# The second step of a double visit moved one visit on, in an attention and SwiGLU kernel on one core

## The chip, the core and the metric

The kernel runs on one core of a Trainium2 chip. The metric is the time of one execution on the device in microseconds, as the median of several runs. The core's engines are named as in the profile: PE is TensorE (matrix products), ACT is ScalarE (activations), DVE is VectorE (elementwise), POOL is GpSimd, and SP is SyncE, which here issues DMAs. Matrix products go to PSUM, the accumulation memory, from which ACT and DVE take them to SBUF.

## The reference

Attention over 8 batches and 12 heads with 448 positions and head size 64, and then a gated feed-forward layer over the 3584 tokens, with width 768 and inner width 1536:

```python
def _attn_ref(q, k, v):
    scores = (1.0 / np.sqrt(q.shape[-1])) * np.matmul(q, k.transpose(0, 1, 3, 2))
    scores = scores - np.max(scores, axis=-1, keepdims=True)
    attn = np.exp(scores)
    attn = attn / (np.sum(attn, axis=-1, keepdims=True) + 1e-09)
    return np.matmul(attn, v)

def _moe_ref(x, w_gate, w_val, w_out):
    g = x @ w_gate
    silu = g * (1.0 / (1.0 + np.exp(-g)))
    val = x @ w_val
    return silu * val @ w_out
```

The input of the feed-forward layer is the attention's output, with the heads side by side.

## The kernel before, in words

The attention is worked off by pairs of heads, 48 of them (six to a batch). The order of the instructions on each engine is written out by hand: every engine takes them in the order in which the program issues them, and semaphores make an engine wait where a tile isn't ready or isn't free. From pair 6 on, the program is a list of *visits* (`plan`, loop over `x`). A visit issues

- the scores of three chunks of keys (`qk`, L356 and L368) into three tiles of the PSUM pool `ps_s`, and for each an exponential on ACT (L378),
- the products with the values for one earlier pair, `todo` (L462), into two tiles of the pool `ps_f`, with the division by the row sums on DVE (`pv_close`, L504 and L505), which writes the pair's slot of a ring of six tiles `xt`,
- the DMA transpose of that pair's result into `X`, the input of the feed-forward layer (`turn_x`, L550, and L556 for the remainder of two pairs),
- the preparation of a later pair's queries and keys (copies on POOL, L240, and a DMA transpose on SP, L244),
- and a share of the feed-forward work of earlier batches.

One visit in seven is *bare*: no pair is due and there are no products with values. The pool `ps_s` has three tiles, each of two banks, and `ps_f` has two of one bank each; a new tile takes the place of the oldest one and waits for its readers.

For the last 33 visits the feed-forward share comes from the table `VISITS`. Its columns are: a block of output work to begin, the number of steps, the number of pairs of output tiles (`run_group`), the number of plain outputs (`run_o`), and the number of sums on DVE (`add_sum`). Rows are numbered here from 0, and "visit 24" means row 24; rows 3, 10, 17, 24 and 31 are bare. A *step* works out 128 columns of the inner layer for one block of tokens, 512 in this part: six matmuls for the gate and six for the value (L610), tanh on ACT, and two multiplications on DVE, of which the last (L696) writes `hts`. A step can be issued in these ways:

- `run_fv`: whole, 512 columns at a time.
- `run_pair`: two steps woven into each other. In a bare visit the first gate goes to a tile of `ps_f` (`gate_small`) and the second to `ps_s`; the second step's value comes in two halves of 256.
- `halves`: gate and value in halves of 256 tokens. The two gate halves take the two banks of one `ps_s` tile, each half has its own tanh (L670) and its own multiplication (L675), and the two value halves take both `ps_f` tiles, each closed by its own L696.

In the loop over the visits, `lone` picks `halves`:

```python
lone = nf == 1 and bool(todo)
...
if lone:
    fvq.pop(0).halves()
    add_sum()
elif bare_next(x):
    for _ in range(nf):
        run_fv()
else:
    run_steps(nf)
```

A *quarter output* is one plain output tile of 128 tokens by 192 columns (`plain_out`, twelve matmuls, L732). It is moved out of PSUM by DVE (L740), or by ACT (L742) in visit 26 (`by_vector`); the last of the four stores the 768 columns. A group in visits 28 and 31 makes two output tiles of 128 tokens out of seven products (L759), after four sums on DVE for each (L593 to L596).

While steps of an old block are left, the transposes of pairs that belong to the next but one block are kept back (`held`), since they overwrite the `X` that those steps read. They are issued at the end of the visit in which the last step was issued. After the last visit, the feed-forward layer of the last four batches follows in units (L929), for which POOL forms sums of weights (L892 to L895) as soon as the attention's buffers come free.

Of the kernel before, what the change touches and what calls it, by code (L numbers as in the profile page):

```python
# [65 lines left out]
def kernel(  # L66
# [959 lines left out]
    with tc.manual_schedule():  # L1026
# [52 lines left out]
        def add_block(i, visits):  # L1079
            if i < B - 2 * NB:  # L1080
                f1, own, n = block(i)
                fvq.extend(f1)
                kk, c0, hts = own
            else:
                own = None
            t_out = NFB * OH / 2400.0
            if i == 0:
                oq.extend([(ffn2_steps(*own, by_half(range(n // 128), OH)), t_out)] * (2 * (n // 128)))
            if i < 2:
                if i:  # L1090
                    ffn2_wait.append(own)
                    sums.extend(wsums)
                    wsums.clear()
                return
            kk, c0, hts = ffn2_wait.pop()
            ffn2_wait.append(own)
            odd = i % 2 == 0
            new = [OutPair(kk, c0, hts, t, 1 - t if i == B - 2 * NB else t) for t in range(1 + odd)]
            groups.extend(new)
            if not odd:  # L1100
                w = QW
                oq.extend([(ffn2_steps(kk, c0, hts, by_half([2], w)), t_out)] * (DM // w))
            for pair in new:
                pair.todo = pair.sums()
                sums.extend(pair.todo)
# [10 lines left out]
        ]  # L1116

        def token_sums(x, w, t, eng=nc.vector):
# [128 lines left out]
        while g < last or queue:  # L1247
            n = 2 if g < WIDE * NC else 3
            todo = []
# [34 lines left out]
        for x, (chunks, todo) in enumerate(plan):  # L1284
# [9 lines left out]
            begins, nf, ng = VISITS[x - base][:3] if x >= base else (0, 0, 0)  # L1294
            if begins > 2:
                add_block(begins, 0)
            lone = nf == 1 and bool(todo)
            behind = []
            for n, (pr, c) in enumerate(ordered if x else []):
                if ng and not todo:  # L1300
# [76 lines left out]
            else:  # L1377
                begins, nf, ng, no, ns = VISITS[x - base]
# [178 lines left out]
```

## Time and profile before

| | us |
|---|---|
| median of 3 runs | 419.69 (419.47 to 420.2) |
| the profiled execution, by the clock of the runs | 420.08 |
| its span, first to last instruction | 418.3 |
| PE busy in the span | 412.2 (99%) |
| DVE, ACT, POOL busy | 273.7, 248.9, 225.4 |
| granted TensorE clock | 1.0 |

The page of the profile gives busy times of each engine and the chain of work that ended last. The timeline gives instructions in order of time, merged where they follow each other on one line of the program: start in microseconds from the start of the span, length, engine, line, operation, the tiles that it writes and reads, and in brackets the idle time before it and what ended that. PE's matmuls overlap, and their ends are modelled, so the distance between starts is the better measure. Visit 24 begins at 232.96 us, visit 31 at 260.17 us.

### The profile page before, as it was taken

How to read it: one execution, taken by the hardware profiler on the slowest of the kernel's cores; microseconds unless marked ns; L12 is line 12 of the kernel's file. 1: busy time of each engine (PE TensorE's matmuls, PEld its weight loads, DVE VectorE, ACT ScalarE, POOL GpSimd, SP SyncE). 2: the span in 40 equal slices, each digit the busy share in tenths (PEclk: the TensorE clock that was granted, in tenths of full speed). 3: DMA queues.
4: the chain of work that ended last, by engine and by line, in shares of the span. 5: the costliest groups of instructions: out<-in, count | busy, mean ns of one | idle time of the engine just before them, and what ended most of it. 6: DMA issues, size and time to landing. Idle time of an engine off the chain costs nothing.

```text
span 418.3 us, 10870 instructions
## 1 busy us (share of the span) xinstructions
PE 412.2 (99%) x4346; PEld 260.4 (62%) x4346; DVE 273.7 (65%) x630; ACT 248.9 (59%) x387; POOL 225.4 (54%) x346
## 2 busy tenths in 40 slices
PE   8999999999999999999999999999999999999996
PEld 3666666655587786786767676555555655555664
DVE  4767562567786674579646578766757665757763
ACT  6975677656677675787656695655453345454121
POOL 8856534998898986398976814599800000000000
PEclk9999999999999999999999999999999999999999
DMA  9999999999999999999999935600000430000225
GB/s 135 192 200 200 200 177 195 129 166 205 196 142 179 153 194 172 154 158 151 167 159 171 102 62 106 186 18 0 2 0 2 121 107 0 2 0 0 76 79 150
DMA packets 108195, 50.29 MB, mean 120 GB/s; under 512 B 60400, under 2 KB 104816, under 8 KB 108144
## 3 DMA queue, kind: packets, MB, share of 16 engines
q0 software_dynamic: 46848, 24.56, 48.3%
q1 hardware_dynamic: 61024, 24.79, 34.7%
q8 instruction: 34, 0.56, 0.6%
q10 hardware_dynamic: 272, 0.25, 0.2%
q14 instruction: 17, 0.14, 0.1%
HBM read 49.55 MB, written 11.01 MB: 145 GB/s over the span
## 4 chain that ended last, share of the span: by engine, by line
PE 94%; DVE 2%; ACT 2%; issue 1%; ACTq 0%; DVEq 0%
PE gp L610 14%; PE un L929 12%; PE vp L610 12%; PE og L759 11%; PE ub L929 10%; PE ob L759 8%; PE acc L462 8%; PE s L356 5%; PE op L732 4%; PE s L393 2%; PE acc L426 2%; PE s L368 1%; PE tp L324 1%; PE wp L166 1%; ACT E L403 1%
## 5 line engine op out<-in xcount | busy, mean ns | idle before, releaser
L378 ACT ACTIVATE E<-s 128x896 f16<-128x896 f32 x126 | 107.4, 916 | 38.2 <-PE s L356 28.0
L610 PE MATMUL gp<-X,wg 128*128 128x256 f16 (+3 forms) x402 | 61.7, 300 | 0.0
L610 PE MATMUL vp<-X,wv 128*128 128x256 f16 (+3 forms) x402 | 58.6, 289 | 0.4 <-DVE xt L505 0.4
L240 POOL COPY qk<-qkraw 128x512 f16<-128x512 f16 x70 | 43.5, 668 | 22.8 <-DMA qkT<-qk 21.7
L180 POOL DMA_DIRECT2D vraw<-in_v_dram x72 | 44.1, 637 | 14.8 <-DMA wo<-in_moe_w_out_dram 8.0
L610 PEld LDWEIGHTS <-wv 128*128 128x128 f16 x444 | 41.6, 98 | 15.3 <-DVE xt L505 0.9
L610 PEld LDWEIGHTS <-wg 128*128 128x128 f16 x402 | 35.5, 98 | 15.8 <-issue 2.2
L180 POOL DMA_DIRECT2D qkraw<-in_k_dram x70 | 42.7, 630 | 4.9 <-DMA wo<-in_moe_w_out_dram 3.5
L403 ACT ACTIVATE E<-s 112x896 f16<-112x896 f32 x48 | 40.7, 918 | 7.5 <-PE s L393 7.5
L462 PEld LDWEIGHTS <-E 128*128 128x128 f16 (+2 forms) x1224 | 38.2, 98 | 8.5 <-issue 3.1
L462 PE MATMUL acc<-vo,E 128*128 128x65 f16 (+2 forms) x1224 | 42.1, 193 | 0.1
L759 PEld LDWEIGHTS <-hts 128*128 128x128 f16 x282 | 27.1, 98 | 17.0
L690 DVE SCALAR_TENSOR_TENSOR t<-sg,gp 128x384 f32<-128x384 f32 (+1 forms) x29 | 17.4, 614 | 24.3 <-ACT sg L637 24.3
L696 DVE SCALAR_TENSOR_TENSOR hts<-t,vp 128x256 f16<-128x256 f32 (+3 forms) x67 | 30.9, 461 | 3.5 <-PE vp L610 1.2
L505 DVE TENSOR_TENSOR xt<-acc,R 128x256 f16<-128x256 f32 x72 | 30.6, 425 | 2.5
L203 POOL DMA_DIRECT2D qkraw<-in_q_dram x44 | 30.2, 685 | 3.0 <-PE s L393 1.0
L356 PE MATMUL s<-qkT 64*64 64x448 f16 (+1 forms) x288 | 28.5, 352 | 0.0
L1002 ACT ACTIVATE silu<-un 128x448 f32<-128x448 f32 x24 | 13.1, 544 | 21.7 <-PE un L929 20.0
L759 PE MATMUL og<-wo,hts 128*128 128x384 f16 x132 | 25.4, 326 | 0.0
L986 DVE TENSOR_TENSOR un<-ub,kept 128x448 f32<-128x448 f32 x24 | 15.1, 631 | 15.6 <-ACT kept L983 10.2
L990 DVE TENSOR_TENSOR kept<-ub,kept 128x448 f32<-128x448 f32 x24 | 15.0, 625 | 13.2 <-PE ub L929 13.2
L979 ACT ACTIVATE ub<-un 128x448 f32<-128x448 f32 x24 | 12.7, 529 | 15.4 <-PE un L929 13.9
(213 smaller groups left out, 748.2 us busy)
## 6 DMA issues: line engine op xcount, KB each, us to landing
vraw<-in_v_dram POOLq DMA_DIRECT2D x72, 64.0 KB, 5.1
qkraw<-in_q_dram POOLq DMA_DIRECT2D x41, 112.0 KB, 4.7
qkraw<-in_k_dram POOLq DMA_DIRECT2D x68, 64.0 KB, 5.0
out_dram<-osb SPq DMA_DIRECT2D x7, 336.0 KB, 3.3
wg<-in_moe_w_gate_dram POOLq DMA_DIRECT2D x8, 288.0 KB, 9.5
wv<-in_moe_w_val_dram POOLq DMA_DIRECT2D x8, 288.0 KB, 10.0
wo<-in_moe_w_out_dram POOLq DMA_DIRECT2D x2, 1152.0 KB, 18.0
out_dram<-osb SPq DMA_DIRECT2D x7, 288.0 KB, 4.9
```

The lines of the kernel that those rows point to most:

```text
L180: eng.dma_start(dst[ts(s, 64)], rows)
L203: nc.gpsimd.dma_start(dst, flat.rearrange("h (p c) d -> p h (c d)", c=NC))
L240: nc.gpsimd.tensor_copy(dst.rearrange("p c h d -> p h c d"), src)
L356: nc.tensor.matmul(s[ts(half, m), hx, 0:S].rearrange("p (c q) -> p c q", q=P), lhsT=t[ts(hx, 64), ds((c + low(pr, hx)) * 128 + half * m, m ...
L378: nc.scalar.activation(e, s[:, :, 0:S], AF.Exp, scale=sm_scale)
L403: nc.scalar.activation(e[:, :, 0:S], s[0:P, :, 0:S], AF.Exp, scale=sm_scale)
L462: nc.tensor.matmul(acc[ds(lo, m), ts((j + pr % 2) % (KR + 1), D + 1)], lhsT=e[rows, ds(hx * S + j * 128 + lo, m)], rhs=Vts[pr % NV][rows, ...
L505: nc.vector.tensor_tensor(xt[:, :, hx], a4[:, :, 0:D], r[:].unsqueeze(2).to_broadcast([128, KR + 1, D]), ALU.mult,)
L610: nc.tensor.matmul(dst[:, 0:w], lhsT=wslice(kind, self.fb, cb), rhs=X[kk][:, cb, ds(c0 + lo, w)], start=(cb == 0), stop=(cb == NCB - 1),)
L696: nc.vector.scalar_tensor_tensor(self.hts[:, self.fb, ds(lo, w)], self.t1[:, ds(lo, w)], 0.5 * HS, vp[:, 0:w], ALU.mult, ALU.mult)
L759: nc.tensor.matmul(dst, lhsT=lhs(n), rhs=rhs(n), start=first and n == 0, stop=n == NH - 1, skip_group_check=True)
L929: mm = nc.tensor.matmul(dst, lhsT=lhs[:, n], rhs=rhs[:, n], start=first and n == 0, stop=n == NK - 1, skip_group_check=True,)
```

## The change

In the table, visit 24 gets one step in place of two, and visit 25 gets the other. The block whose output pairs are used in visits 28 and 31 begins in visit 26 in place of 25, and the four quarter outputs, which were in visits 25, 26, 27 and 29, are now in 26, 27, 29 and 30. The four sums ahead of visit 28 are two in visit 26 and two in visit 27 (before: one, one and two). `lone` no longer asks for a pair that is due, so the single step of the bare visit 24 is issued by `halves` like that of visit 25. No other bare visit has a single step.

```diff
@@ VISITS, rows 20 to 32
             (0, 0, 1, 0, 0), (0, 1, 0, 0, 0), (0, 1, 0, 0, 0), (0, 1, 0, 0, 0),
-            (0, 2, 0, 0, 0),
-            (4, 0, 0, 1, 1), (0, 0, 0, 1, 1), (0, 0, 0, 1, 2), (0, 0, 1, 0, 0), (0, 0, 0, 1, 2),
-            (0, 0, 0, 0, 0), (0, 0, 1, 0, 0), (0, 0, 0, 0, 0),
+            (0, 1, 0, 0, 0),
+            (0, 1, 0, 0, 0), (4, 0, 0, 1, 2), (0, 0, 0, 1, 2), (0, 0, 1, 0, 0), (0, 0, 0, 1, 2),
+            (0, 0, 0, 1, 0), (0, 0, 1, 0, 0), (0, 0, 0, 0, 0),
         ]
@@ loop over the visits
             begins, nf, ng = VISITS[x - base][:3] if x >= base else (0, 0, 0)
             if begins > 2:
                 add_block(begins, 0)
-            lone = nf == 1 and bool(todo)
+            lone = nf == 1
             behind = []
```

2 rows, old and new, of the table VISITS are left out of this document.

## The prediction

> **What bounds the kernel now.** I read the head of the page first, then the timeline of TensorE over the visits that the change touches, then that of ScalarE, VectorE and SyncE beside it.
>
> ```profile
> span 418.3 us, 10870 instructions
> PE 412.2 (99%) x4346; PEld 260.4 (62%) x4346; DVE 273.7 (65%) x630; ACT 248.9 (59%) x387; POOL 225.4 (54%) x346
> PE 94%; DVE 2%; ACT 2%; issue 1%; ACTq 0%; DVEq 0%
> L378 ACT ACTIVATE E<-s 128x896 f16<-128x896 f32 x126 | 107.4, 916 | 38.2 <-PE s L356 28.0
> ```
>
> TensorE is busy for 99% of the span and is 94% of the chain that ended last. So whatever lengthens the stream of matmuls, or stops it, is paid in full; the other engines matter only where TensorE waits for them. An exponential (L378) takes 916 ns. The profiled execution took 420.08 us by the clock of the runs, 1.78 us outside its span of 418.3, and lies 0.39 us over the median of 419.69; I work out a difference from its rows and add it to the median.
>
> Now TensorE. Columns: start, length, engine, line and operation. The ends of matmuls are modelled, so I use distances between starts only.
>
> ```profile
> 228.71 0.74 PE L356 MATMUL s<-qkT 64*128 64x448 f16 x6
> 229.29 1.12 PE L462 MATMUL acc<-vo,E 64*128 64x65 f16 x32
> 230.24 1.47 PE L610 MATMUL gp<-X,wg 128*128 128x256 f16 x12
> 231.55 1.47 PE L610 MATMUL vp<-X,wv 128*128 128x256 f16 x12
> 232.96 0.38 PE L368 MATMUL s<-qkT 64*64 64x448 f16 x4
> 233.65 2.76 PE L610 MATMUL gp<-X,wg 128*128 128x512 f16 x12
> 236.25 1.46 PE L610 MATMUL vp<-X,wv 128*128 128x512 f16 x6
> 238.95 0.74 PE L356 MATMUL s<-qkT 64*128 64x448 f16 x6
> 239.53 1.12 PE L462 MATMUL acc<-vo,E 64*128 64x65 f16 x32
> 240.49 1.15 PE L732 MATMUL op<-wo,hts 128*128 128x192 f16 x12
> 241.57 0.38 PE L368 MATMUL s<-qkT 64*64 64x448 f16 x4
> 241.94 0.57 PE L356 MATMUL s<-qkT 64*64 64x448 f16 x8
> 242.32 1.16 PE L462 MATMUL acc<-vo,E 64*64 64x65 f16 x40
> 243.31 1.15 PE L732 MATMUL op<-wo,hts 128*128 128x192 f16 x12
> 244.40 0.85 PE L356 MATMUL s<-qkT 64*128 64x448 f16 x6
> 247.13 0.38 PE L368 MATMUL s<-qkT 64*64 64x448 f16 x4
> 258.50 0.88 PE L356 MATMUL s<-qkT 64*128 64x448 f16 x6
> 259.20 1.13 PE L462 MATMUL acc<-vo,E 64*128 64x65 f16 x32
> 260.17 1.14 PE L759 MATMUL og<-wo,hts 128*128 128x384 f16 x6
> ```
>
> The reader sees one visit after another, each beginning with scores (L356 or L368). Visit 23 begins at 228.71: scores 0.58, products of a pair 0.95, then a step in halves, 2.72 up to the next visit (230.24 to 232.96). Visit 24 at 232.96 is the double one: scores 0.69, no products, then both steps in 5.30 (233.65 to 238.95). Visit 25 (238.95) has products and a quarter output, visits 26 (241.57) and 27 (244.40) the same, visit 28 (247.13) a pair of output tiles, visit 30 (258.50) scores and products alone. There is no long hole here to be filled: the visits follow each other with waits of a tenth of a microsecond. What the change can gain is small, then, and the question is whether it opens a hole.
>
> **The change part by part.** A. *Matmuls.* Before, the two steps are 18 matmuls of 512 columns and 12 of 256; after, 48 of 256. Twelve of 512 are 236.25 less 233.65, 2.60 us or 217 ns each; twelve of 256 are 231.55 less 230.24, 1.31 us or 109 ns each. So a split costs next to nothing, and most of the rest is that a step that stands alone ends at a change of shape: two steps at 2.72 are 5.44 against 5.30, **+0.14**.
>
> The Trainium skill, page TensorE: Matmul & The Clock Gate, section Back-to-back issue gap, speaks against halves: it gives a sustained spacing of about 131 ns at 512 columns and 81 at 128, against an isolated gap of N/2.4 + 2.5 ns. By the first, a matmul of 256 would be an estimated 98 ns, two of them 65 ns over one of 512, and the 18 splits 1.2 us. The rows above contradict it (217 and 109 ns) and follow the isolated gap.
>
> B. *The quarter outputs.* One leaves visit 25 (240.49 to 241.57, 1.08) and one comes to visit 30, between products and `og`: 1.08 in, **0**. The other three stay in visits 26, 27 and 29. Visit 30 has room on VectorE for the eviction, and the store goes to SyncE two transposes later; the buffer that it empties is next written by the first output tile after the attention.
>
> C. *The gate of visit 24 waits for an exponential.* This is the large term. ScalarE:
>
> ```profile
> 231.52 0.68 ACT L670 ACTIVATE sg<-gp 128x256 f32<-128x256 f32 x2
> 233.42 2.54 ACT L378 ACTIVATE E<-s 128x896 f16<-128x896 f32 x3 [1.22 <-PE s L368]
> 235.83 1.22 ACT L637 ACTIVATE sg<-gp 128x512 f32<-128x512 f32 x2
> 239.36 5.18 ACT L378 ACTIVATE E<-s 128x896 f16<-128x896 f32 x6 [2.31 <-PE s L356]
> 244.50 0.33 ACT L742 ACTIVATE osb<-op 128x192 f32<-128x192 f32 x1
> ```
>
> Before, `run_pair` puts the first gate of a bare visit into `ps_f`, free at that moment, and it starts at 233.65 as soon as the scores are issued. `halves` always takes a tile of `ps_s`, of which there are three; the visit's three score tiles come just ahead of it, so it gets the first of them, when its exponential has read it. In an ordinary visit 0.95 us of products lie between and hide this (visit 23: scores 228.71, gate 230.24). Visit 24 has none. Its first exponential starts at 233.42 and takes 0.92, to 234.34. How fast TensorE follows: of the six exponentials from 239.36, the third ends 2.54 after the first starts (as in 233.42's group), at 241.90, and the scores that wait for it start at 241.94. So the gate starts at 234.38 in place of 233.65: **+0.73**. Queued behind it is all of TensorE's work.
>
> D. *The products of visit 25 wait for the closing multiplications.* VectorE, and then SyncE's queue, which E needs (the last two rows are landings, least, median and most, of L556 from 215 to 275 us and of the transposes into X from 242.5 to 247):
>
> ```profile
> 232.63 0.86 DVE L696 SCALAR_TENSOR_TENSOR hts<-t,vp 128x256 f16<-128x256 f32 x2
> 246.09 0.42 DVE L505 TENSOR_TENSOR xt<-acc,R 128x256 f16<-128x256 f32 x1
> 246.64 0.42 DVE L505 TENSOR_TENSOR xt<-acc,R 128x256 f16<-128x256 f32 x1
> 247.23 0.36 DVE L740 TENSOR_SCALAR osb<-op 128x192 f32<-128x192 f32 x1 [0.17 <-PE op L732]
> 239.05 2.48 SPq L550 DMA_TRANSPOSE X<-xt  x2
> 241.58 1.23 SPq L556 DMA_TRANSPOSE X<-xt  x1
> 244.20 2.29 SPq L550 DMA_TRANSPOSE X<-xt  x1
> X<-xt SPq DMA_TRANSPOSE x18, 2.4
> DMA to landing us min/median/max: 2.3/2.4/3.1
> DMA to landing us min/median/max: 2.3/2.9/4.1
> ```
>
> In visit 23 the first tanh starts at 231.52 and the second L696 ends at 233.49, 1.97 later. In visit 24 the exponentials let the first tanh start at 235.83, so the second L696 ends at 237.80, and the two `ps_f` banks that it reads are what the products of visit 25 need, from 237.84. TensorE would be there at 234.38 + 2.72 + 0.58 = 237.68: **+0.16**. From there visit 25 runs as visit 23 did: products 0.95, step 2.72, visit 26 at 241.51 (before 241.57, with a quarter output more done).
>
> E. *SyncE's queue and the ring of six `xt`.* The transposes of pairs 36 to 39 are held until the last step has read the old X. They start at 239.05 now, 0.10 after the visit that follows the step; after the change at 241.61, with pair 40's among them. The third, L556 for 36 and 37, is issued 2.53 behind the first (241.58), so at 244.14, and lands 2.4 later, at 246.5. Pair 42 writes the slot of 36: its first L505 stands at 246.09 now (visit 27 plus 1.69). After, visit 27 starts at 241.51 + 0.69 + 0.99 + 1.09 = 244.28 and that L505 is due at 245.97: it waits 0.55. Behind it on VectorE lie the other L505 (to 247.5) and the eviction L740, then from about 247.5 to 247.83; and visit 28's third score tile, due 0.45 into that visit at 247.46, needs the bank that L740 frees, at 247.87: **+0.41**. Bounds: 0 if the landing is 0.5 earlier, some 2.1 if it takes 4.1, as one transpose of this stretch does (the last row; SyncE's row at 244.20, 2.29 long, is that one). The keys' transpose of pair 46 goes ahead of the held ones, that of 47 about 0.8 earlier than now; GpSimd, which waits for these to form weight sums, gets no later.
>
> F. *What stops being late.* In visit 26 the scores take 0.75 (241.57 to 242.32) because the exponentials run through from visit 25; after it, with a long visit 25, 0.69: **-0.06**. Visit 27's scores wait now for L742 (to 244.83); after, the exponentials of visit 26 end at about 244.5 again, so that stays. VectorE gets a sum (L593) one visit later, where it has room.
>
> Sum: 0.14 + 0 + 0.73 + 0.16 + 0.41 - 0.06 = 1.38 us, about +1.3, with E the soft one. On the profiled execution 421.4; on the median **421.0 us**. Everything after visit 30 is the same work at the same distances, only later.
>
> **The rivals.** *E does not come.* The landing is a little quicker, or VectorE's delay finds slack. Then 0.97 us remain: 420.7. For it: 0.5 us decides and the slack before is 2 us. Against: the row of 2.4 is steady.
>
> *Not slower.* The gate of visit 24 does not wait: if the first exponential has freed its bank by 233.65, 0.7 us earlier than its row allows, or the pool hands out another bank, C and D vanish; with E gone too, 0.14 - 0.06 is left, 419.8. For it: TensorE shows no idle time here and steady visits hide exactly this wait. Against: the built program puts a wait on ScalarE at this gate, where before's waits for VectorE. If in addition the small waits at visits 26, 27 and 30 (0.06; 0.09 of 0.67 in the scores of 244.40; 0.12 of 0.70 in those of 258.50, against 0.58) all went, 419.5; a gain of more than 0.84 has no row to come from, and I keep a small chance for what I don't see.
>
> *Slower still.* The transposes land late, 4.1 as above: 1.8 more, 422.8. Decided by whether L505 of pair 42 gets past 247.
>
> *Halves cost TensorE more than half.* By the page's figures this is 1.2 us more; as a mechanism of this kernel the rows bound it by A, and it is already in the steps of visit 23. I give it 2 in 100, within the case above.
>
> **How the numbers follow.** A measurement here tells about 0.2% from no change: 0.84 us, so 418.85 and 420.53 are the limits. Forecast with E 0.45; without E 0.22, of which 0.08 may fall inside the limit; not slower 0.20; faster than 418.85 0.06; later transposes and costly halves 0.07. Faster 0.06; same 0.20 + 0.08 = 0.28; slower 0.66. The range from 419.6 to 422.0 holds the forecast, the case without E and most of the one that is not slower.
>
> **What would show it.** Right: in visit 24 TensorE idle before the first `gp` half for about 0.7 us, released by the exponential; the first products of visit 25 released by L696; visit 26 starting within 0.2 us of 241.57; L505 of pair 42 released by a DMA at about 246.5; visit 30 to `og` 1.08 longer. Wrong: the first gate half within 0.1 us of the scores, or two steps over 5.6 us without a wait, or a time below 419.6.

## The result, and the profile after

The changed kernel takes 421.63 us in the median of six runs (421.0 to 421.89), against 419.67 for the kernel before: a ratio of 1.0042, interval 1.0032 to 1.0052. It is 1.96 us slower; the forecast was 1.3 us slower, 421.0 us, within 419.6 to 422.0. The profiled execution took 421.83, 420.1 of it in its span.

The stretch from visit 23 to the first output product (`og`) of visit 31 holds the whole change. It is cut here at the starts of visits 26, 27, 28, 29 and 30, first before, then after (the columns are the stretch, its length, and the busy time and instructions of PE, PEld, DVE, ACT and POOL, then the granted clock, DMA share and GB/s):

```profile
228.71:241.57 12.86, 12.86 (x155) 8.71 (x154) 7.50 (x21) 8.93 (x13) 9.59 (x15) 1.00 0.95 104
241.57:244.40 2.83, 2.83 (x66) 2.31 (x66) 2.39 (x8) 2.71 (x4) 0.69 (x1) 1.00 0.35 70
244.40:247.13 2.73, 2.73 (x52) 2.16 (x52) 1.73 (x6) 2.70 (x5) 0.00 (x0) 1.00 0.27 52
247.13:255.75 8.62, 8.62 (x97) 5.35 (x96) 5.72 (x13) 4.17 (x7) 1.78 (x2) 1.00 0.55 84
255.75:258.50 2.75, 2.75 (x52) 2.13 (x52) 2.56 (x7) 2.29 (x3) 1.49 (x2) 1.00 0.52 104
258.50:260.17 1.67, 1.67 (x39) 1.23 (x39) 1.53 (x4) 1.45 (x3) 0.69 (x2) 1.00 0.16 33
```

```profile
228.37:241.05 12.68, 12.01 (x162) 9.50 (x161) 7.64 (x23) 9.27 (x15) 9.79 (x15) 1.00 1.04 112
241.05:243.70 2.65, 2.65 (x65) 2.24 (x64) 1.84 (x8) 2.22 (x3) 2.29 (x3) 1.00 0.23 46
243.70:246.54 2.84, 2.84 (x52) 2.16 (x51) 1.35 (x4) 2.84 (x5) 0.00 (x0) 1.00 0.22 43
246.54:256.51 9.97, 8.70 (x95) 5.35 (x95) 6.07 (x16) 4.28 (x7) 0.00 (x0) 1.00 0.35 69
256.51:259.26 2.75, 2.75 (x51) 2.13 (x50) 2.56 (x7) 2.28 (x3) 1.66 (x2) 1.00 0.46 92
259.26:261.93 2.67, 2.67 (x52) 2.23 (x51) 2.46 (x7) 2.45 (x4) 1.69 (x3) 1.00 0.51 122
```

The stretch is 31.46 before and 33.56 after, 2.10 longer. Visits 23 to 25 are 0.18 shorter with a quarter output (1.08) less in them, so 0.90 is lost there; visit 26 gains 0.18, visit 27 loses 0.11, visit 28 loses 1.35, and visit 30 is 1.00 longer with the quarter. What follows `og` is 158.13 us before and 158.17 after: nothing. (What precedes visit 23 was 0.34 shorter in this execution, hence 1.8 in the spans.)

Two rows have TensorE less busy than the stretch is long, by 0.67 and by 1.27. The waits of TensorE between 228 and 272 us in the changed kernel (who waited for whom, total, times, longest; the kernel before has none there) and the rows around them, with the two of ScalarE that visit 24's step depends on:

```profile
PE s L356 <- DVE osb L740: 1.3, 1, 1.3
PE gp L610 <- ACT E L378: 0.7, 1, 0.7
232.82 0.55 PE L356 MATMUL s<-qkT 64*64 64x448 f16 x8
234.04 1.47 PE L610 MATMUL gp<-X,wg 128*128 128x256 f16 x12 [0.67 <-ACT E L378]
235.35 1.47 PE L610 MATMUL vp<-X,wv 128*128 128x256 f16 x12
236.75 0.74 PE L356 MATMUL s<-qkT 64*128 64x448 f16 x6
237.33 1.17 PE L462 MATMUL acc<-vo,E 64*128 64x65 f16 x32
238.34 1.47 PE L610 MATMUL gp<-X,wg 128*128 128x256 f16 x12
248.41 0.38 PE L356 MATMUL s<-qkT 64*64 64x448 f16 x4 [1.27 <-DVE osb L740]
233.07 2.54 ACT L378 ACTIVATE E<-s 128x896 f16<-128x896 f32 x3 [1.21 <-PE s L368]
235.48 0.68 ACT L670 ACTIVATE sg<-gp 128x256 f32<-128x256 f32 x2
```

The gate of visit 24 waits for its exponential as forecast (C). The third score tile of visit 28 waits for the eviction L740. Why that is late stands on VectorE and SyncE (the first row belongs to visit 24, and the last two are the landings of the transposes issued at 241.15 and 242.42):

```profile
236.59 0.75 DVE L696 SCALAR_TENSOR_TENSOR hts<-t,vp 128x256 f16<-128x256 f32 x2
247.12 0.42 DVE L505 TENSOR_TENSOR xt<-acc,R 128x256 f16<-128x256 f32 x1 [1.65 <-DMA X<-xt]
247.67 0.42 DVE L505 TENSOR_TENSOR xt<-acc,R 128x256 f16<-128x256 f32 x1
248.01 0.35 DVE L740 TENSOR_SCALAR osb<-op 128x192 f32<-128x192 f32 x1
242.42 2.20 SPq L550 DMA_TRANSPOSE X<-xt  x1
244.67 1.23 SPq L556 DMA_TRANSPOSE X<-xt  x1
DMA to landing us min/median/max: 4.1/4.1/4.1
DMA to landing us min/median/max: 3.3/3.3/3.3
```

L505 of pair 42 waits 1.65 us for a transpose into X, and L740 follows behind it. The held transposes start at 241.15, the second (242.42) holds SyncE for 2.20 in place of 1.2, and the third, L556, is issued at 244.67, 3.52 behind the first where I had 2.53. The first lands after 4.1 and the second after 3.3, not 2.3. This is E, three times its forecast size.

### The profile page after: what moved, and what is told of

The parts are those of the page before. It is cut to its first block, busy times and chain, and to the rows that moved or that the text cites. A ratio compares the mean times of both kernels' runs of the same rounds, so it can differ in the third digit from the quotient of the medians.

```text
span 420.1 us, 10913 instructions
## 1 busy us (share of the span) xinstructions
PE 412.2 (98%) x4364; PEld 261.8 (62%) x4364; DVE 269.6 (64%) x633; ACT 248.7 (59%) x389; POOL 226.0 (54%) x346
## 4 chain that ended last, share of the span: by engine, by line
PE 93%; DVE 2%; DMA 1%; ACT 1%; issue 0%; SPq 0%; DVEq 0%
PE gp L610 14%; PE un L929 12%; PE vp L610 12%; PE og L759 11%; PE ub L929 9%; PE ob L759 8%; PE acc L462 8%; PE s L356 5%; PE op L732 3%; PE s L393 2%; PE acc L426 2%; PE s L368 1%; PE tp L324 1%; ACT E L403 1%; DMA rk<-in_k_dram 1%; PE acc L434 1%
## 5 line engine op out<-in xcount | busy, mean ns | idle before, releaser
L610 PEld LDWEIGHTS <-wg 128*128 128x128 f16 x414 | 36.7, 98 | 15.6 <-issue 2.8
L696 DVE SCALAR_TENSOR_TENSOR hts<-t,vp 128x256 f16<-128x256 f32 (+3 forms) x69 | 31.3, 455 | 3.3 <-PE vp L610 0.9
L505 DVE TENSOR_TENSOR xt<-acc,R 128x256 f16<-128x256 f32 x72 | 30.6, 425 | 4.1 <-DMA X<-xt 1.6
L690 DVE SCALAR_TENSOR_TENSOR t<-sg,gp 128x384 f32<-128x384 f32 (+1 forms) x27 | 16.1, 608 | 23.1 <-ACT sg L637 23.1
L675 DVE SCALAR_TENSOR_TENSOR t<-sg,gp 128x256 f32<-128x256 f32 (+1 forms) x42 | 15.5, 394 | 10.9 <-ACT sg L670 9.9
```

The source lines that it names most:

```text
L505: nc.vector.tensor_tensor(xt[:, :, hx], a4[:, :, 0:D], r[:].unsqueeze(2).to_broadcast([128, KR + 1, D]), ALU.mult,)
L610: nc.tensor.matmul(dst[:, 0:w], lhsT=wslice(kind, self.fb, cb), rhs=X[kk][:, cb, ds(c0 + lo, w)], start=(cb == 0), stop=(cb == NCB - 1),)
L696: nc.vector.scalar_tensor_tensor(self.hts[:, self.fb, ds(lo, w)], self.t1[:, ds(lo, w)], 0.5 * HS, vp[:, 0:w], ALU.mult, ALU.mult)
```

## The experiments

All differences are to the kernel before. "Stretch" is from visit 23 to `og` of visit 31 in the profile; the times are medians, with the ratio to the kernel before on the same chip. That ratio is the one on record and not the quotient of the medians; the two differ most for shift, where two of ten times are near 425.

| kernel | stretch, us | time, us | ratio (interval) |
|---|---|---|---|
| changed kernel | +2.10 | 421.63 | 1.0042 (1.0032 to 1.0052) |
| ring8 | +0.74 | 420.45 | 1.0021 (1.0009 to 1.0033) |
| whole24 | +1.96 | 422.23 | 1.0062 (1.0050 to 1.0074) |
| steps_only | +1.21 | 420.91 | 1.0030 (1.0018 to 1.0042) |
| quarters_only | +0.81 | 420.28 | 1.0018 (1.0008 to 1.0027) |
| before_ring8 | +0.01 | 419.53 | 1.0001 (0.9992 to 1.0010) |
| swap24_ring8 | +0.52 | 420.41 | 1.0020 (1.0011 to 1.0030) |
| shift | +1.12 | 421.10 | 1.0052 (1.0027 to 1.0078) |

The median of the kernel before was 419.51 beside the first four experiments and 419.47 beside the last three. My theory was that the loss has two places: visit 24, as long as ScalarE's and VectorE's work on it (C, D), and the ring of `xt` behind SyncE's transposes (E).

**ring8: the ring's wait taken away.**

```diff
-NX = 6
+NX = 8
```

> The changed kernel with eight slots for the pairs' results (xt) in place of six, so that pair 42 writes a slot whose transposes were done long ago; nothing else differs. My theory: in visit 27 L505 waited 1.65 us for the third held transpose, the eviction L740 queued behind it, and TensorE stood 1.27 us at visit 28's third score tile. Then both waits go and the kernel gains about 1.2 us: some 420.4 us, 0.7 to 0.9 over the kernel before. Rival: the 1.27 us come from VectorE's load, which has two sums (L593, L594) in visit 26 now, or from ScalarE; then the wait stays and the time is 421.6.

420.45, as the theory had it. TensorE's one wait left in the stretch is that of visit 24, and L505 of pair 42 follows the division's first instruction at once:

```profile
245.33 0.18 DVE L504 RECIPROCAL R<-acc 128x4 f32<-128x4 f32 x1 [0.38 <-PE acc L462]
245.55 0.43 DVE L505 TENSOR_TENSOR xt<-acc,R 128x256 f16<-128x256 f32 x1
246.80 0.68 PE L356 MATMUL s<-qkT 64*64 64x448 f16 x8
```

The sums are in visit 26 here as well, so VectorE's load isn't the cause; the rival falls.

**before_ring8: the same edit on the kernel before.**

> The kernel before with eight slots for the pairs' results in place of six: the control for the run with eight slots on the changed kernel. My theory: in the kernel before no instruction waits for a slot (the third held transpose lands about 2 us ahead of pair 42's L505), so the time stays within 0.2 us of the kernel before. Rival: the larger ring helps by something else, as fewer waits on VectorE or SyncE throughout; then this gains too, up to the 1.0 us that the changed kernel gained from it.

No difference (1.0001). The longer ring helps only where a transpose is late, so the 1.35 us of visit 28 that it takes away are the change's.

**whole24: the step of visit 24 whole, with another bank for its gate.**

```diff
-            lone = nf == 1
+            lone = nf == 1 and bool(todo)
```

> The changed kernel, but the single step of the bare visit 24 is issued whole (512 columns), its gate in a ps_f tile; visit 25 keeps halves. My theory: visit 24 is as long as ScalarE's three exponentials, the tanh behind them and VectorE's closing multiplications; the 0.67 us wait ahead of the gate goes, but the products of visit 25 then wait for L696, which ends about 237.4 on the changed kernel's clock against 237.33 for their start now. So the wait moves by 2.7 us and the time stays within 0.3 us of 421.6. Rival: the wait is only one for a bank of ps_s, and another bank saves its 0.67 us: 420.9.

The wait moved, as expected. TensorE's waits in the stretch, and the products of visit 25:

```profile
PE s L356 <- DVE osb L740: 0.8, 1, 0.8
PE acc L462 <- DVE hts L696: 0.6, 1, 0.6
237.10 0.69 DVE L696 SCALAR_TENSOR_TENSOR hts<-t,vp 128x512 f16<-128x512 f32 x1
237.84 1.11 PE L462 MATMUL acc<-vo,E 64*128 64x65 f16 x31 [0.60 <-DVE hts L696]
```

The gate follows the scores at once, and the products stop at their second accumulator until L696 has read the value. The edit changes two things, the bank and the step's halves, and together they save nothing: the stretch is +1.96 against +2.10, but the wait for L740 is 0.42 smaller here, so without that it would be 0.28 longer. No run has the other bank alone. The times are 0.6 over the changed kernel's, with intervals that overlap; the profile has no place for that, and I can't say whether it is real.

**swap24_ring8: gates in `ps_f`, values in `ps_s`, and the third exponential behind the tanh, in visit 24.**

```diff
-                late = late or n == 2 and lone and not fvq[0].at[1]
+                late = late or n == 2 and lone and (not todo or not fvq[0].at[1])
...
+            if bare:
+                gates = [ps_f.tile([128, 512], FP32, tag="f", name="gp") for _ in parts]
...
+            if bare:
+                vs = ps_s.tile([128, 2, 512], FP32, tag="s", name="vp")
+                vps = [vs[:, i] for i in range(2)]
```

> The changed kernel with eight slots and, in the bare visit 24 alone, three edits to the step in halves: its gate halves take the two ps_f tiles, its value halves the two banks of a ps_s tile, and the third exponential of the visit is issued behind the two tanh. My theory: what is left over the kernel before in the run with eight slots (0.74 us in the profile, 0.9 in the times) is the visit whose step waits for ScalarE's three exponentials, the tanh and VectorE behind them. With the gates free of the exponentials and the tanh 0.8 us earlier, the gate follows the scores at once and the products of visit 25 start 0.4 to 0.7 us earlier: 419.9 to 420.1 in the times of the first job. Rival: only the place of a bank matters or only the order on ScalarE does, and the other takes over: gain below 0.2 us.

A miss. The gate's wait goes and the tanh starts at 234.79, but the next wait stands ready (the edit moves L670 to L674 and L696 to L704):

```profile
234.79 0.67 ACT L674 ACTIVATE sg<-gp 128x256 f32<-128x256 f32 x2
236.25 0.75 DVE L704 SCALAR_TENSOR_TENSOR hts<-t,vp 128x256 f16<-128x256 f32 x2 [0.28 <-PE vp L610]
237.05 0.36 PE L356 MATMUL s<-qkT 64*128 64x448 f16 x2 [0.36 <-DVE hts L704]
```

The closing multiplication waits for both value halves, which share a tile now, and the third scores of visit 25 need that tile. The stretch is 0.22 shorter than in ring8, not 0.4 to 0.7; that is nearer to the rival's limit of 0.2, and the times don't tell the two runs apart. So the wait ahead of the gate is not by itself worth its 0.67 us. My reading is that the chain behind it sets the length: from the first exponential to the end of the second closing multiplication it takes 4.27 us in the changed kernel (233.07 to 237.34) and 3.82 here, and the matmuls of the visit take 3.4 (scores 0.69, step 2.71).

**steps_only and quarters_only: the two halves of the change.** The rows of the table are, from visit 24 on,

```diff
 steps_only
+            (0, 1, 0, 0, 0),
+            (4, 1, 0, 1, 1), (0, 0, 0, 1, 1), (0, 0, 0, 1, 2), (0, 0, 1, 0, 0), (0, 0, 0, 1, 2),
+            (0, 0, 0, 0, 0), (0, 0, 1, 0, 0), (0, 0, 0, 0, 0),
 quarters_only
+            (0, 2, 0, 0, 0),
+            (0, 0, 0, 0, 0), (4, 0, 0, 1, 2), (0, 0, 0, 1, 2), (0, 0, 1, 0, 0), (0, 0, 0, 1, 2),
+            (0, 0, 0, 1, 0), (0, 0, 1, 0, 0), (0, 0, 0, 0, 0),
```

> Only the steps are moved (one in visit 24, one in visit 25, both in halves); the quarter outputs, the block begin and the sums stay in visits 25, 26, 27 and 29 as before. My theory: the loss in visit 24 stays (0.14 for shapes, 0.67 for the gate, 0.06 for the products, about 0.9 with 0.06 given back), but visit 25 is 1.1 us longer, so the transposes of pairs 36 and 37 have landed, or nearly, when pair 42 wants their slot: TensorE waits 0 to 0.2 us in visit 28 in place of 1.27. Time about 420.6. Rival: if visit 30's new quarter or visit 25's missing one is what costs, this comes out near the kernel before, 419.7; if the step's place alone costs everything, 421.6.

> Only the quarter outputs, the block begin and the sums are moved; both steps stay woven in visit 24 as before, so visit 25 has scores and products alone. My theory: the quarter in visit 25 covered the exponentials; without it the scores of visit 26 wait for the bank of visit 25's third exponential (free at about 241.9 on the clock of before) while TensorE would be there at 240.5, so nearly all of the 1.08 us taken out of visit 25 is waited for, and visit 30 is 1.08 longer: about 0.9 us over before, 420.6. The held transposes start as before, no wait for xt. Rival: visits are bound by matmuls alone, and the quarter costs the same in either place: 419.7.

Waits of TensorE in the stretch, steps_only first, with two rows of its VectorE, then quarters_only with rows of its visits 25 and 26:

```profile
PE gp L610 <- ACT E L378: 0.7, 1, 0.7
PE s L356 <- DVE osb L740: 0.4, 1, 0.4
241.47 1.17 DVE L593 TENSOR_TENSOR qkraw<-hts 128x768 f16<-128x768 f16 x1
242.57 0.34 DVE L740 TENSOR_SCALAR osb<-op 128x192 f32<-128x192 f32 x1
```

```profile
PE s L356 <- ACT E L378: 0.6, 2, 0.4
238.84 1.12 PE L462 MATMUL acc<-vo,E 64*128 64x65 f16 x32
239.89 0.38 PE L368 MATMUL s<-qkT 64*64 64x448 f16 x4
241.25 0.38 PE L356 MATMUL s<-qkT 64*64 64x448 f16 x4 [0.43 <-ACT E L378]
```

In steps_only the loss of visit 24 is there and visit 28 has no wait: pair 42's L505 comes 1.4 us later (246.93, against 245.50 where it was due in the changed kernel), and the third held transpose has landed by then, at about 246.8. The total is 0.3 over the expectation, for a wait that I had not seen: the first sum (L593) stands ahead of the eviction of visit 25's quarter, and the scores of visit 26 wait 0.37. The edit does a little more than move the steps here: the branch for a single step calls `add_sum()` too, so visit 25 has two sums where the kernel before has one, and the 0.37 is a cost of this run that the changed kernel, where no sums are due yet in visit 25, doesn't have.

In quarters_only the scores of visit 26 wait twice for exponentials of visit 25, 0.6 together, and the stretch is 0.81 longer, about as expected (0.9). Visits 25 and 26 are only 0.20 shorter without the quarter (5.25 against 5.45), and visit 30 is 1.00 longer with it: where the quarter stood it cost 0.20, since the exponentials needed its time. Neither half of the change gains. That 1.21 and 0.81 add up to nearly the whole's 2.10 is chance: the waits are others.

**shift: the fetch of instructions moved away from the transposes.** It leaves the computation alone.

```diff
-        dummy(7)
+        wp = ps_f.tile([128, 512], FP32, tag="f", name="wp")
+        for _ in range(56):
+            nc.tensor.matmul(wp[:, 0:64], lhsT=warm[:], rhs=warm[:, 0:64], start=True, stop=True)
```

> The changed kernel with 49 more (narrow) matmuls and weight loads in the warm-up at the very start, in the place of wider ones; nothing near visit 24 differs. It moves the points at which TensorE's instructions are fetched (packets of 16 KB on the queue of kind instruction, one per 256 instructions) by 98 instructions, some 3.7 us earlier. My theory: the second of the held transposes took 2.2 us in place of 1.2, and landed 1 us later, since such a packet, from 242.9 us, shares the DMA engines with it; with the packet near 239 the third held transpose lands 2.3 to 2.4 after its issue, L505 of pair 42 waits about 0.7 us in place of 1.65 and TensorE 0.4 in place of 1.27, and the time from visit 23 to the output pair of visit 31 is 0.9 us shorter than in the changed kernel. Rival: the transposes are slow for what they move or for the queue that they stand in, whatever the packet; then the wait of 1.27 us stays.

The packet moved, and with it the slow transpose. First the changed kernel's instruction packet between 242.5 and 243 us, then that of shift between 241 and 241.5 (its visit 23 starts 1.42 later, so the packet comes 2.9 earlier in the work, 3.7 were expected), and its rows:

```profile
q8 instruction: 1, 0.02, 17.2%
```

```profile
q8 instruction: 1, 0.02, 15.3%
242.57 2.48 SPq L550 DMA_TRANSPOSE X<-xt  x2
245.11 1.23 SPq L556 DMA_TRANSPOSE X<-xt  x1
247.56 0.43 DVE L505 TENSOR_TENSOR xt<-acc,R 128x256 f16<-128x256 f32 x1 [0.66 <-DMA X<-xt]
248.85 0.38 PE L356 MATMUL s<-qkT 64*64 64x448 f16 x4 [0.28 <-DVE osb L740]
```

The first two transposes take 2.48 together in place of 3.47, L556 is issued 2.54 behind the first, L505 waits 0.66, TensorE 0.28, and the stretch is 0.98 shorter than in the changed kernel, close to the expectation (0.7, 0.4 and 0.9). Its times scatter more (420.51 to 425.28), and what precedes visit 23 is 1.42 longer, so they don't show this by themselves.

## Why the prediction was right, and where it was off

Point by point, by its own letters:

- **A** and **D** with **C**, forecast 1.03 together: measured 0.90. The two steps without their waits take 5.42, 0.12 more than before (0.14 forecast). The gate starts 1.43 after the scores (232.61 to 234.04) where it was 0.69, so it comes 0.74 later (0.73 forecast); the 0.67 of the profile is the idle time alone. The products of visit 25 start as soon as their scores are done and lose 0.06, not 0.16, because the second L696 ends at 237.34, when they are due, 1.86 behind the first tanh (235.48) and not 1.97 as in visit 23. The profile lists no wait there, so the sign that I had named, these products released by L696, did not come. In whole24 that wait is there, 0.60, but behind a step that is whole.
- **B**, forecast 0: out 1.08, in 1.00. But I priced it as if the quarter were movable at will. quarters_only shows that in visit 25 it covered exponentials; in the change, where the scores of visit 26 wait for nothing, the moved step took over that cover.
- **E**, forecast 0.41 and called the soft term: 1.27 by the wait and 1.35 by visit 28. This is the step that was mis-sized, and it and not C became the large term. The mechanism was right, down to the instruction that waits; the interval from the first to the third transpose was taken from the one fast case of the trace before (2.53) and was 3.52. L505 of pair 42 came 1.65 late where I had 0.55. The slow case was in the trace, and I kept it for the upper bound alone. (I also put the landing of 4.1 to the transpose at 244.20; it belongs to the one ahead of it, at 242.90, and that at 244.20 lands after 3.4. And the last transpose of keys, which I had 0.8 earlier, is issued 0.6 later, 254.30 against 253.69; what follows `og` is no longer for it.)
- **F**, forecast -0.06: visit 26 gained 0.18 and visit 27 lost 0.11. That the two come to -0.07 is luck. In visit 27 I had the wait for L742 unchanged; L742 ends 0.54 into the visit now and ended 0.43 into it before, which is the 0.11.

The sum of 1.38 became 2.10 in the profile, 0.94 more for E and 0.22 less for the rest. Of the rivals, the one that was not slower fell at the first row: the gate did wait. "E does not come" is what ring8 measures, and its figure of 0.97 compares with 0.74 in the profile and 0.94 in the times. "Slower still", which with the costly halves had 7 in 100, came in part: its sign was L505 of pair 42 past 247, and that starts at 247.12 here, 247.46 with visit 23 set to the same start. It cost 0.94 of the 1.8 us that I gave it, and the time stayed in the range because the rest was smaller and the range reached to 422.0.

The Trainium skill's sustained spacing (TensorE: Matmul & The Clock Gate, Back-to-back issue gap), by which halves would have cost an estimated 1.2 us more, is contradicted once more: the new step takes 1.31 for its twelve gate matmuls of 256 columns (234.04 to 235.35), as visit 23 did before.

No version that has the change or a part of it reaches the kernel before; the best, quarters_only, is 0.18% slower.

## What to carry to other kernels

Work that sits in a stretch may be there as cover: before moving it, ask which engine's chain passes under it, and give the stretch that loses it the length of that chain, not of its matmuls. A wait removed by another bank can come back at the next reader, as it did in both runs here, when the chain behind it is what sets the time. And a transfer that is delayed by the change must be followed to the reuse of its source buffer, with the slowest landing of the trace and not the usual one.

## What the runs showed of the hardware

An instruction fetch can slow a DMA transpose that is in flight. The page counts 34 packets on the instruction queue, 0.56 MB or 16 KB each, for the 8728 matmuls and weight loads of TensorE, which makes one for about 257 instructions; that they are TensorE's is borne out by shift, which changed only the number of these. In each of the eight kernels other than shift such a packet falls between 242.7 and 244.4 us; the held transpose that is in flight then lands after 3.5 to 4.2 us in place of 2.3, and the next one keeps SyncE for 1.8 to 2.4 in place of 1.2. In shift the packet came before the first of them, and the first three took the usual time; the slow ones there are those issued at 247.73 and 248.98 (landing after 4.0, SyncE held for 2.14), around the next packet at 249.55. The packet of the kernel before, between 243.8 and 244 us:

```profile
q8 instruction: 1, 0.02, 47.2%
```

There it came behind the first three held transposes, issued from 239.05 to 241.58, and met the two after them. The change issues the first three from 241.15 on, and the packet between 242.8 and 243 meets the first two: this is what made E's interval 3.52 and not 2.53. Why a packet of 16 KB delays a transpose by more than its own time (it takes 1.4 us in the changed kernel, the first transpose lands 1.8 later), no run shows. Which transpose is hit depends on the number of instructions before it, so an edit elsewhere can change it.
